# Cached attention with output projection on one core: a V block in two transfers, the last unit's turn moved ahead of the wo products, half of wo in one transfer, x in 16 rows

## The chip, the cores and the metric

The kernel runs on one core of a Trainium2 chip. The metric is the device time of one execution in microseconds (us). Other times are from one profiled execution and count from the start of its span.

The engines are called PE (matrix products; PEld is its weight load), DVE (vector), ACT (scalar), POOL and SP (which issues the DMA transfers here). The core's transfers run on 16 DMA engines.

## The reference

Eight sequences of four new tokens attend to a cache of 2048 keys and values. There are 32 query heads and 8 key/value heads of size 128; four query heads share one key/value head.

```
q = (x @ wq)                      # x [8, 4, 512], wq [512, 4096]
scores = q . k_cache * 128**-0.5  # k_cache [8, 8, 2048, 128]
p = softmax(scores)
o = p . v_cache                   # v_cache [8, 8, 2048, 128]
out = o @ wo                      # wo [4096, 512], out [8, 4, 512]
```

All arrays are bf16. K and V are 32 MiB each, wq and wo 4 MiB each, x 32 KiB: about 75.5 MB are read, and 32 KiB written.

## The kernel before, in words

The work is cut into 16 units: one sequence and four key/value heads each. A unit has 64 rows of queries (four heads, four query heads each, four tokens). K is loaded in eight transfers of 4 MiB, one for each sequence (`load_pair`, L95), that is for two units; V in blocks of 2 MiB, one for each unit (`load_v`, L100), of which the first two come as one transfer (L149). The sequence positions are spread over the partitions, so that each transfer writes 128 partitions in long runs.

For each pair of units DVE turns the K block in four pieces (`turn_keys`, L129), PE makes the scores from them (L227), DVE finds the maxima and ACT the exponentials with their sums (`softmax_top`, L245 to L263), DVE turns these (`turn_probs`, L276), and copies on ACT, POOL and DVE spread them into an array that PE can use as weights (`copy_probs`, L290). PE multiplies them with the V block in 32 products of 256 columns, in four quarters (`values`, L328). A unit's result is then divided by the sums (`divide`, L342, on ACT, for the last units on DVE), turned by a product with an identity matrix and copied into the array oT (`finish`, L352: the product at L365, for unit 15 two at L357; a copy at L366). `all_values(w, ...)` (L483) runs the four quarters of unit w, with whatever functions are handed to it after the first, second, third and fourth quarter.

When all units of one half of the heads are in oT (units that belong to the first half end with unit 13, those of the second with unit 15), `to_tokens(n)` (L373) turns that half to rows of tokens with eight products into two PSUM tiles and copies these to nat_sb with ACT and DVE; `to_wo_rows(n)` (L388) takes every eighth column of it with eight more products and copies the result to oP with ACT and DVE. `project(p, r0, n)` (L406) then multiplies rows r0 to r0+n-1 of the piece p of oP with wo: two products of 256 columns for each row, one for either half of the output. wo comes in six transfers (`pieces`, L417): two pieces of 1 MiB for the first half of the heads, and 1 MiB, 640, 256 and 128 KiB for the second half. The products go into two PSUM tiles (out_ps) that two copies (L555) take to out_sb, and one transfer stores it (L556).

The order of the instructions on each engine is that of the program text (`manual_schedule`, L71): every engine runs its own in the order in which they are written. All transfers are issued by SP, in order. SP waits before a transfer until the buffer is free, and in the trace also until a transfer further back has landed. The first wo transfer is issued at 156.03 us, when PE has read the last V block in the buffer that wo takes over; the last at 159.90 us.

The tail, from L532 on, is this: unit 12's values; unit 13's, with finish(12) inside; divide(13) on ACT; finish(13); unit 14's values, with to_tokens(0) after the first quarter and to_wo_rows(0) after the third; divide(14) on DVE; unit 15's values, with finish(14) after the second quarter; divide_all(15) on ACT; then wo products between the steps of unit 15's turn:

```
    project(0, 0, half)
    finish(NU - 1)
    project(0, half, half)
    to_tokens(1)
    project(1, 0, half)
    to_wo_rows(1)
    project(1, half, half)
    for piece in pieces[2:]:
        project(*piece)
```

x is loaded near the start (L112 to L114). With XR = 4 it lies in 8 partitions, four tokens of 1 KiB in a row, in the buffer that later takes the first V block; DVE clears this part of the buffer first, and 16 small products turn x (L141).

Of the kernel before, what the change touches and what calls it, by code (L numbers as in the profile page):

```python
# [14 lines left out]
def kernel(  # L15
# [9 lines left out]
    nc = tc.nc  # L25
# [8 lines left out]
    G = 4  # L34
    S = 128 // G
    C = Sk // S
# [5 lines left out]
    HP = 8  # L42
    WR = 8
    NP = Hq // HP
    DH = D // 2
    NU = (Hkv // G) * B
    KB, VB, PB, LAG = 2, 2, 2, 2
    NPAIR = NU // 2
    XR = 4
    scale = float(Dh) ** -0.5  # L50
    AX = mybir.AxisListType.X
    ADD = mybir.AluOpType.add
# [37 lines left out]
    vs = [v_sb[u % VB] for u in range(NU)]  # L90
# [4 lines left out]
    def load_pair(p):  # L95
        nc.sync.dma_start(
            k_sb[p % KB][:, :, :], k_cache[p].rearrange("g (s c) d -> (g s) c d", c=CP)
        )

    def load_v(u):  # L100
        v, b = units[u]
        nc.sync.dma_start(
            vs[u], v_cache[b, G * v : G * v + G].rearrange("g (s c) d -> (g s) c d", c=C)
        )

    def load_wo(p, r0, n):
        rows = wo[p * HP * 128 : (p + 1) * HP * 128, :].rearrange("(q r) j -> q r j", r=WR)
        w0 = p * WR + r0
        nc.sync.dma_start(wo_sb[:, w0 : w0 + n, :], rows[:, r0 : r0 + n, :])

    load_pair(0)
    x_all = v_sb[0][:T, :, :].rearrange("q c d -> q (c d)")[:, : XR * D]  # L112
    nc.vector.memset(x_all, 0.0)
    nc.sync.dma_start(x_all[::XR, :], x.flatten_outer_dims().rearrange("(a i) d -> a (i d)", i=XR))  # L114
    nc.sync.dma_start(wq_sb[:, :, :], wq.rearrange("(p r) n -> p r n", r=R))
# [21 lines left out]
    xtp = psum_m.tile([128, R, T], FP32, tag="m", name="xtp")  # L137
    for i in range(XR):
        row = x_all[:, i * D : (i + 1) * D].rearrange("q (p r) -> q r p", r=R)
        for r in range(R):  # L140
            nc.tensor.matmul(  # L141
                xtp[:, r, i::XR],
                lhsT=row[:, r, :],
                rhs=ident[:T, :T:XR],
                start=True,
# [153 lines left out]
    def sums(p):  # L299
        swapped = []  # L300
        for j in range(2):
            swapped.append(small.tile([128, 1], FP32, tag=f"l_swapped{j}", name="l_swapped"))
            swap_halves(nc.gpsimd, swapped[j], l_sbs[(p, j)])
        found = []
        for v in range(2):
            total = small.tile([128, 1], FP32, tag=f"l_total{v}", name="l_total")
            for i in range(4):
                rows, j = slice(i * S, (i + 1) * S), (i % 2) ^ v
                nc.gpsimd.tensor_tensor(  # L309
                    out=total[rows, :], in0=l_sbs[(p, j)][rows, :], in1=swapped[j][rows, :], op=ADD  # L310
                )
            found.append((units.index((v, p)), total))
        return found
# [8 lines left out]
    def values(u, quarter):  # L322
        if quarter == 0:
            o_pss[u] = psum_o.tile([128, 2, Dh], FP32, tag="o", name="o_ps")
        h, a0 = quarter // 2, quarter % 2 * (C // 8)
        for a in range(C // 8):
            c = quarter * C // 4 + 2 * a
            nc.tensor.matmul(  # L328
                o_pss[u][:, :, :].rearrange("n j d -> n (j d)"),
                lhsT=probs_of[u][:, h, a0 + a, :, :, :].rearrange(  # L330
                    "s j g q -> s (j g q)"
                ),
                rhs=vs[u][:, c : c + 2, :].rearrange("s c d -> s (c d)"),
                start=(c == 0),
                stop=(c == C - 2),
            )

    def divide_all(u):
        o_scs[u] = const.tile([128, 2, Dh], FP32, name="o_all")
        nc.scalar.mul(out=o_scs[u][:, :, :], in_=o_pss[u][:, :, :], mul=r_sbs[u][:, 0:1])  # L340

    def divide(u):  # L342
        o_scs[u] = small.tile([128, Dh], FP32, tag="o_sc", name="o_sc")
        for h in range(2):
            rows = slice(h * NQ, (h + 1) * NQ)
            to, of, by = o_scs[u][rows, :], o_pss[u][rows, h, :], r_sbs[u][rows, 0:1]
            if u < NU - LAG:
                nc.scalar.mul(out=to, in_=of, mul=by)  # L348
            else:
                nc.vector.tensor_scalar_mul(out=to, in0=of, scalar1=by)  # L350

    def finish(u):  # L352
        v, b = units[u]
        o_t = psum_m.tile([128, NQ], FP32, tag="m", name="o_t")
        if u == NU - 1:
            for h in range(2):
                nc.tensor.matmul(  # L357
                    o_t[:, :],
                    lhsT=o_scs[u][:, h, :],
                    rhs=ident4[:, h * NQ : (h + 1) * NQ],  # L360
                    start=(h == 0),
                    stop=(h == 1),
                )
        else:
            nc.tensor.matmul(o_t[:, :], lhsT=o_scs[u][:, :], rhs=both[:, :], start=True, stop=True)  # L365
        (nc.scalar.copy if u in (NU - 3, NU - 1) else nc.vector.tensor_copy)(  # L366
            out=oT[v][:, :, :, b, :].rearrange("d (k r) p s -> d p k r s", k=2),
            in_=o_t[:, :].rearrange("d (k p r s) -> d p k r s", k=2, p=2, s=Sq),
        )
# [3 lines left out]
    def to_tokens(n):  # L373
        half = HP // 2
        for i, copy in enumerate(two_copies):
            nat = psum_m.tile([2 * T, half, 128], BF16, tag="m", name="nat")
            for h in range(half):
                nc.tensor.transpose(  # L378
                    nat[:, h, :],
                    oT[n][:, (i ^ n) * half + h, :, :, :].rearrange("d p b s -> d (p b s)"),  # L380
                    ident[:, :],
                )
            copy(
                out=nat_sb[:, i * half * 128 : (i + 1) * half * 128],
                in_=nat[:, :, :].rearrange("t h d -> t (h d)"),
            )

    def to_wo_rows(n):  # L388
        by_row = nat_sb[:, :].rearrange("t (q r) -> t r q", r=WR)
        half = WR // 2  # L390
        for i, copy in enumerate(two_copies):
            perm = psum_m.tile([128, half, 2 * T], FP32, tag="m", name="perm")
            for r in range(half):
                nc.tensor.matmul(  # L394
                    perm[:, r, :],
                    lhsT=by_row[:, i * half + r, :],
                    rhs=ident[: 2 * T, : 2 * T],
                    start=True,
                    stop=True,
                )  # L400
            copy(
                out=oP[n][:, i * half : (i + 1) * half, :, :].rearrange("q r p t -> q r (p t)"),
                in_=perm[:, :, :],
            )

    def project(p, r0, n):  # L406
        for r in range(r0, r0 + n):
            for half in range(2):
                nc.tensor.matmul(  # L409
                    out_ps[half][half * T : (half + 1) * T, :],  # L410
                    lhsT=oP[p // 2][:, r, p % 2, :],
                    rhs=wo_sb[:, p * WR + r, half * DH : (half + 1) * DH],
                    start=(p == 0 and r == 0),
                    stop=(p == NP - 1 and r == WR - 1),
                )

    pieces = [(0, 0, 8), (1, 0, 8), (2, 0, 8), (3, 0, 5), (3, 5, 2), (3, 7, 1)]  # L417

    waiting = []

    def all_inverses():
        while waiting:
            inverses(*waiting.pop(0))
# [59 lines left out]
    def all_values(w, *between):  # L483
        for quarter in range(4):
            values(w, quarter)
            for what in between[quarter : quarter + 1]:
                if what:
                    what()

    p, w = NPAIR - 1, NU - 7  # L490
# [28 lines left out]
    all_values(w + 1)  # L519
    divide(w + 1)  # L520
    load_v(NU - 2)
    load_v(NU - 1)
    waiting += sums(p)
    all_values(NU - 5, None, lambda: finish(NU - 7))
    divide(NU - 5)
# [1 line left out]
    copy_probs(NU - 2, (nc.gpsimd.tensor_copy,))  # L527
    all_inverses()
    wo_sb = wpool.tile([128, NP * WR, D], BF16, tag="w", name="wo_sb")
    for piece in pieces:  # L530
        load_wo(*piece)
    all_values(NU - 4, lambda: finish(NU - 6), lambda: finish(NU - 5))  # L532
# [1 line left out]
    copy_probs(NU - 1, act_dve)  # L534
    all_values(NU - 3, None, lambda: finish(NU - 4))
    divide(NU - 3)
    finish(NU - 3)
    all_values(NU - 2, lambda: to_tokens(0), None, lambda: to_wo_rows(0))
    divide(NU - 2)
    all_values(NU - 1, None, lambda: finish(NU - 2))  # L540
    divide_all(NU - 1)

    out_ps = [psum_s.tile([128, DH], FP32, tag="s", name="out_ps") for _ in range(2)]
    half = WR // 2
    project(0, 0, half)
    finish(NU - 1)
    project(0, half, half)
    to_tokens(1)
    project(1, 0, half)
    to_wo_rows(1)  # L550
    project(1, half, half)
    for piece in pieces[2:]:
        project(*piece)
    for i, copy in enumerate((nc.scalar.copy, nc.vector.tensor_copy)):
        copy(out=out_sb[:, i * DH : (i + 1) * DH], in_=out_ps[i][i * T : (i + 1) * T, :])  # L555
# [31 lines left out]
```

## Time and profile before

| | us |
|---|---|
| device time, median of 3 runs | 184.58 (184.46 to 184.69) |
| device time of the profiled execution | 184.57 |
| its span | 182.70 |

| engine | busy us | share of the span |
|---|---|---|
| PE | 147.6 | 81% |
| PEld | 90.8 | 50% |
| DVE | 128.2 | 70% |
| ACT | 73.8 | 40% |
| POOL | 69.0 | 38% |

The mean granted clock of PE over the span is 0.981 of full speed. 75.73 MB are moved, at a mean of 415 GB/s.

A line of a timeline gives the start in us, the time taken in us, the engine, the line of the kernel, the operation, out<-in with the names of the tiles, the shapes, and the number of instructions merged into the line. Brackets hold the idle time of that engine just before, and what ended it. A line of the DMA issues gives out<-in, the issuing engine, the number of transfers, the KB of each and the median time from issue to landing. The page's row of slices cuts the span into 40 equal parts; a digit is the busy share in tenths, 9 is 90% or more. A busy PE is not PE at its peak, since products are pipelined: the time from one start to the next is what counts.

### The profile page before, as it was taken

How to read it: one execution, taken by the hardware profiler on the slowest of the kernel's cores; microseconds unless marked ns; L12 is line 12 of the kernel's file. 1: busy time of each engine (PE TensorE's matmuls, PEld its weight loads, DVE VectorE, ACT ScalarE, POOL GpSimd, SP SyncE). 2: the span in 40 equal slices, each digit the busy share in tenths (PEclk: the TensorE clock that was granted, in tenths of full speed). 3: DMA queues.
4: the chain of work that ended last, by engine and by line, in shares of the span. 5: the costliest groups of instructions: out<-in, count | busy, mean ns of one | idle time of the engine just before them, and what ended most of it. 6: DMA issues, size and time to landing. Idle time of an engine off the chain costs nothing.

```text
span 182.7 us, 2731 instructions
## 1 busy us (share of the span) xinstructions
PE 147.6 (81%) x1032; PEld 90.8 (50%) x1032; DVE 128.2 (70%) x170; ACT 73.8 (40%) x129; POOL 69.0 (38%) x171
## 2 busy tenths in 40 slices
PE   0019549996799799987498998978998999989993
PEld 0014114433343384563156656835853579877872
DVE  6019365879779788929799897799859659960210
ACT  2000050088060059500920892891496068682030
POOL 8900040038331237411331381572363399860000
PEclk9999996999999999999789999999999999999999
DMA  6998999999989999999989999999999999999991
GB/s 230 459 431 387 452 459 398 416 438 466 452 370 441 459 398 475 396 427 470 441 377 434 457 441 395 431 423 484 398 416 427 438 431 427 431 427 416 429 389 45
DMA packets 4524, 75.73 MB, mean 415 GB/s; under 512 B 504, under 2 KB 664, under 8 KB 928
## 3 DMA queue, kind: packets, MB, share of 16 engines
q1 hardware_dynamic: 4512, 75.57, 96.9%
q8 instruction: 8, 0.13, 0.3%
q14 instruction: 4, 0.03, 0.0%
HBM read 75.53 MB, written 0.03 MB: 414 GB/s over the span
## 4 chain that ended last, share of the span: by engine, by line
DMA 42%; DVE 30%; PE 14%; issue 6%; ACT 4%; POOL 1%; SPq 1%; ACTq 0%; DVEq 0%
DMA k_sb<-in_k_cache_dram 27%; DVE kt L129 21%; DMA k_sb<-in_v_cache_dram 16%; PE o_ps L328 8%; DVE top L245 5%; ACT s_sb L263 3%; PE s_ps L227 2%; PE out_ps L409 2%; DVE p_t L276 2%; DVE swapped L237 1%; ACT probs L290 1%; DVE less L251 1%; PE perm L394 1%; POOL probs L290 1%; PE nat L378 1%
## 5 line engine op out<-in xcount | busy, mean ns | idle before, releaser
L129 DVE STREAM_TRANSPOSE kt<-k_sb 128x2048 f32<-128x2048 f32 x32 | 71.5, 2278 | 16.3 <-DMA k_sb<-in_k_cache_dram 13.9
L328 PEld LDWEIGHTS <-probs 128*128 128x128 bf16 x448 | 42.4, 99 | 15.2 <-issue 8.2
L227 PE MATMUL s_ps<-kt,q_bd 128*64 128x512 bf16 x256 | 36.9, 403 | 15.1 <-DVE kt L129 8.9
L263 ACT ACTIVATE s_sb<-s_ps,less 128x1024 bf16<-128x1024 f32 x16 | 22.4, 1401 | 58.5 <-DVE less L251 26.6
L290 POOL COPY probs<-p_t 32x512 bf16<-32x512 bf16 x48 | 29.1, 606 | 34.0 <-PE o_ps L328 31.9
L157 PE MATMUL unread<-ident 128*128 128x512 f32 (+1 forms) x86 | 40.0, 610 | 0.0
L290 ACT COPY probs<-p_t 32x512 bf16<-32x512 bf16 x52 | 32.0, 616 | 1.3 <-DVE p_t L276 0.3
L227 PEld LDWEIGHTS <-q_bd 128*64 128x64 bf16 x256 | 15.7, 112 | 32.9 <-issue 18.9
L157 PEld LDWEIGHTS unread<-ident 128*128 128x128 f32 x86 | 16.2, 198 | 18.6 <-issue 18.5
L328 PE MATMUL o_ps<-v_both,probs 128*128 128x256 bf16 x192 | 23.0, 273 | 0.9 <-DMA v_both<-in_v_cache_dram 0.8
L245 DVE TENSOR_REDUCE top<-s_ps 128x1 f32<-128x1024 f32 x16 | 19.4, 1212 | 4.7 <-PE s_ps L227 4.7
L328 PE MATMUL o_ps<-v_more,probs 128*128 128x256 bf16 x160 | 19.8, 277 | 0.0
L237 POOL COPY l_swapped<-l_sb 64x1 f32<-64x1 f32 x32 | 6.5, 204 | 32.2 <-ACT s_sb L263 31.3
L276 DVE STREAM_TRANSPOSE p_t<-s_sb 128x512 f32<-128x512 f32 x16 | 11.3, 708 | 6.0 <-ACT s_sb L263 6.0
L348 ACT ACTIVATE o_sc<-o_ps,r_sb 64x128 f32<-64x128 f32 x28 | 10.1, 360 | 10.9 <-PE o_t L365 7.7
L309 POOL TENSOR_TENSOR l_total<-l_sb,l_swapped 32x1 f32<-32x1 f32 x64 | 11.8, 184 | 4.0
L328 PE MATMUL o_ps<-k_sb,probs 128*128 128x256 bf16 x96 | 11.6, 272 | 0.2 <-DMA k_sb<-in_v_cache_dram 0.2
L141 PE MATMUL xtp<-ident,v_both 32*128 32x8 bf16 x16 | 0.7, 174 | 13.1 <-DMA v_both<-in_x_dram 13.1
L181 ACT ACTIVATE q_nat<-psq 128x512 bf16<-128x512 f32 x2 | 1.2, 598 | 22.1 <-PE psq L170 22.1
L290 POOL COPY last_probs<-p_t 32x512 bf16<-32x512 bf16 x12 | 8.1, 673 | 0.6
L196 POOL COPY q_bd<-q_t 32x512 bf16<-32x512 bf16 x3 | 1.9, 646 | 16.7 <-DVE q_t L190 16.6
L290 DVE COPY probs<-p_t 32x512 bf16<-32x512 bf16 x12 | 7.9, 661 | 0.3
(47 smaller groups left out, 83.9 us busy)
## 6 DMA issues: line engine op xcount, KB each, us to landing
k_sb<-in_k_cache_dram SPq DMA_DIRECT2D x8, 4096.0 KB, 19.9
v_more<-in_v_cache_dram SPq DMA_DIRECT2D x6, 2048.0 KB, 25.0
v_both<-in_v_cache_dram SPq DMA_DIRECT2D x4, 2048.0 KB, 22.6
k_sb<-in_v_cache_dram SPq DMA_DIRECT2D x4, 2048.0 KB, 24.8
wq_sb<-in_wq_dram SPq DMA_DIRECT2D x1, 4096.0 KB, 19.9
v_both<-in_v_cache_dram SPq DMA_DIRECT2D x1, 4096.0 KB, 29.6
wo_sb<-in_wo_dram SPq DMA_DIRECT2D x3, 1024.0 KB, 19.1
wo_sb<-in_wo_dram SPq DMA_DIRECT2D x1, 640.0 KB, 21.1
```

The source lines that it names most:

```text
L129: nc.vector.transpose(kts[(p, t)][:, :, :, :, :, :].rearrange("k c w j s e -> k (c w j s e)").bitcast(FP32), k_sb[p % KB][:, t * CT : (t + ...
L157: nc.tensor.matmul(unread[:, :, :], lhsT=ident4[:, :], rhs=ident4[:, :].unsqueeze(1).broadcast_to([128, width, 128]), start=True, stop=True,)
L227: nc.tensor.matmul(s_pss[(p, j)][h * NQ : (h + 1) * NQ, t // 2, :, :], lhsT=q_bd[:, j, k, e, p, :, :].rearrange("k g q -> k (g q)"), rhs=k ...
L237: engine.tensor_copy(out=out[h * NQ : (h + 1) * NQ, :], in_=in_[(1 - h) * NQ : (2 - h) * NQ, :])
L245: nc.vector.reduce_max(out=top[:, :], in_=s_pss[u][:, :, :, :].rearrange("q i c s -> q (i c s)"), axis=AX,)
L263: nc.scalar.activation(out=s_sbs[u][:, :, :, :].rearrange("q a w j -> q a j w"), in_=s_pss[u][:, :, :, :].rearrange("q i c s -> q c s i"), ...
L276: nc.vector.transpose(p_ts[u][:, :, :, :, :].rearrange("s x g q j -> s (x g q j)").bitcast(FP32), s_sbs[u][:, :, :, :].rearrange("q a s j ...
L290: by[x * G + col](out=probs_of[u][rows, x, :, :, col, :], in_=p_ts[(b, j)][quad * S : (quad + 1) * S, :, col % 2, :, :].rearrange("s x q j ...
L309: nc.gpsimd.tensor_tensor(out=total[rows, :], in0=l_sbs[(p, j)][rows, :], in1=swapped[j][rows, :], op=ADD)
L328: nc.tensor.matmul(o_pss[u][:, :, :].rearrange("n j d -> n (j d)"), lhsT=probs_of[u][:, h, a0 + a, :, :, :].rearrange("s j g q -> s (j g q)"),
L348: nc.scalar.mul(out=to, in_=of, mul=by)
L409: nc.tensor.matmul(out_ps[half][half * T : (half + 1) * T, :], lhsT=oP[p // 2][:, r, p % 2, :], rhs=wo_sb[:, p * WR + r, half * DH : (half ...
```

## The change

Four things change.

- x is laid in 16 partitions with two tokens in each (XR = 2), and so in rows of 2 KiB; the cleared part of the buffer and the number of products that turn it follow from XR.
- Unit 15's V block is loaded in two transfers, the first and the second half of the runs of each partition. The other blocks are loaded as before.
- The two wo pieces of the first half of the heads are loaded in one transfer of 2 MiB; the runs of 8 KiB are the same. The other four pieces stay.
- In the tail, finish(13) moves into unit 14's values, after the second quarter; to_tokens(0) moves from after the first quarter to after the third, and to_wo_rows(0) from after the third quarter to behind divide(14). After unit 15's values the turn of unit 15 (finish, to_tokens) comes at once. Four of the sixteen rows of the first half's wo products (eight products) stay between to_tokens(1) and to_wo_rows(1), all others come after to_wo_rows(1).

```diff
-    XR = 4
+    XR = 2
...
-    def load_v(u):
+    def load_v(u, c0=0, n=C):
         v, b = units[u]
-        nc.sync.dma_start(
-            vs[u], v_cache[b, G * v : G * v + G].rearrange("g (s c) d -> (g s) c d", c=C)
-        )
+        blocks = v_cache[b, G * v : G * v + G].rearrange("g (s c) d -> (g s) c d", c=C)
+        nc.sync.dma_start(vs[u][:, c0 : c0 + n, :], blocks[:, c0 : c0 + n, :])
...
+    def load_first_half_of_wo():
+        p = NP // 2
+        nc.sync.dma_start(
+            wo_sb[:, : p * WR, :].rearrange("q (p r) j -> q p (r j)", p=p),
+            wo[: p * HP * 128, :].rearrange("(p q r) j -> q p (r j)", p=p, r=WR),
+        )
...
-    pieces = [(0, 0, 8), (1, 0, 8), (2, 0, 8), (3, 0, 5), (3, 5, 2), (3, 7, 1)]
+    pieces = [(2, 0, 8), (3, 0, 5), (3, 5, 2), (3, 7, 1)]
...
     load_v(NU - 2)
-    load_v(NU - 1)
+    for c0 in (0, C // 2):
+        load_v(NU - 1, c0, C // 2)
...
     wo_sb = wpool.tile([128, NP * WR, D], BF16, tag="w", name="wo_sb")
+    load_first_half_of_wo()
     for piece in pieces:
         load_wo(*piece)
...
     divide(NU - 3)
-    finish(NU - 3)
-    all_values(NU - 2, lambda: to_tokens(0), None, lambda: to_wo_rows(0))
+    all_values(NU - 2, None, lambda: finish(NU - 3), lambda: to_tokens(0))
     divide(NU - 2)
+    to_wo_rows(0)
     all_values(NU - 1, None, lambda: finish(NU - 2))
     divide_all(NU - 1)
 
     out_ps = [psum_s.tile([128, DH], FP32, tag="s", name="out_ps") for _ in range(2)]
-    half = WR // 2
-    project(0, 0, half)
     finish(NU - 1)
-    project(0, half, half)
     to_tokens(1)
-    project(1, 0, half)
+    project(0, 0, WR // 2)
     to_wo_rows(1)
-    project(1, half, half)
-    for piece in pieces[2:]:
+    project(0, WR // 2, WR // 2)
+    project(1, 0, WR)
+    for piece in pieces:
         project(*piece)
```

## The prediction, made before the changed kernel ran

> **What bounds the kernel now.** I read the page first: engine shares, the slices, the DMA queues.
>
> ```profile
> DMA  6998999999989999999989999999999999999991
> ...
> q1 hardware_dynamic: 4512, 75.57, 96.9%
> q8 instruction: 8, 0.13, 0.3%
> ```
>
> The DMA row is full in 38 of 40 slices, and the loads' queue takes 96.9% of sixteen engines' span. So the time can change in two ways only: the bytes take longer or shorter, or something happens behind the last landing. I therefore went to the end, first with the DMA issues and their times to landing in narrow windows (line, size in KB, us from issue to landing).
>
> ```profile
> k_sb<-in_v_cache_dram SPq DMA_DIRECT2D x1, 2048.0 KB, 24.7
> ```
>
> ```profile
> wo_sb<-in_wo_dram SPq DMA_DIRECT2D x1, 128.0 KB, 19.6
> ```
>
> The first is unit 14's V block, issued at 140.00: it lands at 164.7. Unit 15's, issued at 144.83, takes 24.8: 169.6. The second is the last wo piece, issued at 159.90: it lands at 179.5. The same view gives the wo pieces before it: 174.5 for (1,0,8), 177.0 for (2,0,8), 178.5 for (3,0,5), 179.1 for (3,5,2). Then the timeline of the tail (start, us, engine, line; in brackets the idle time before).
>
> ```profile
> 160.02 1.91 PE L328 MATMUL o_ps<-k_sb,probs 128*128 128x256 bf16 x16 [0.19 <-DMA k_sb<-in_v_cache_dram]
> ...
> 164.72 0.43 PE L365 MATMUL o_t<-both,o_sc 128*128 128x64 f32 x2 [0.88 <-ACT o_sc L348]
> ...
> 164.99 1.04 PE L328 MATMUL o_ps<-k_sb,last_probs 128*128 128x256 bf16 x8
> ...
> 169.88 1.91 PE L328 MATMUL o_ps<-k_sb,probs 128*128 128x256 bf16 x16
> ...
> 173.63 0.61 PE L409 MATMUL out_ps<-wo_sb,oP 128*32 128x256 bf16 x8
> 173.74 0.48 ACT L340 ACTIVATE o_all<-o_ps,r_sb 128x256 f32<-128x256 f32 x1 [4.52 <-PE o_ps L328]
> ...
> 174.27 0.66 PE L357 MATMUL o_t<-ident,o_all 128*128 128x64 f32 x4
> ...
> 174.96 0.21 ACT L366 CAST oT<-o_t 128x64 bf16<-128x64 f32 x1 [0.75 <-PE o_t L357]
> ...
> 175.40 0.63 PE L378 MATMUL nat<-ident,oT 128*64 128x128 bf16 x8
> ...
> 175.90 0.58 ACT L383 COPY nat_sb<-nat 64x512 bf16<-64x512 bf16 x1 [0.73 <-PE nat L378]
> ...
> 176.63 0.66 PE L394 MATMUL perm<-ident,nat_sb 64*128 64x64 bf16 x8
> ...
> 177.22 2.56 PE L409 MATMUL out_ps<-wo_sb,oP 128*32 128x256 bf16 x40
> ...
> 179.50 0.09 PEld L409 LDWEIGHTS <-oP 128*32 128x32 bf16 x1 [0.17 <-issue]
> 179.80 0.36 ACT L555 CAST out_sb<-out_ps 32x256 bf16<-32x256 f32 x1 [2.35 <-PE out_ps L409]
> ```
>
> The reader is to see that two limits meet here. The last pair of wo products starts at 179.50, when the last piece lands. But PE was almost as late: from 164.99 on it hardly pauses, and the last 40 products (20 pairs, since each row r has one for either half of the output, and the two run side by side) start at 177.22 and follow each other at 0.109 us a pair, as the trace's single records show. Unhindered, the twentieth would start at 177.23 + 19 x 0.109 = 179.30. So **PE's slack against the last landing is 0.2 us**: whatever PE does later than 0.2 us is paid in full, whatever it does earlier is worth nothing beyond the landing.
>
> **The change, part by part.** All is reckoned against the profiled execution, span 182.70 and 184.57 us in all; the median of the runs is 184.58, so a difference carries over directly.
>
> *Order in the tail.* Prices first. A value product takes 0.109 us ((1.91 - 0.27) / 15 from the row of 16). A finish between values costs 0.17 (171.62 to 171.79). to_tokens(0) costs 0.66 (164.99 + 8 x 0.109 = 165.87; the next value row is at 166.53), to_wo_rows(0) 0.72 (166.53 + 16 x 0.109 = 168.27 to 168.99).
> 1. finish(13) leaves the head of unit 14. PE now goes from unit 13 straight to unit 14's V block. That lands at 164.73; unit 13's landed at 159.88 and its first product started at 160.02, so unit 14 starts at about 164.87 instead of 164.99: 0.12 earlier. (Bounds: nothing gained, or 0.2.)
> 2. finish(13) comes back inside unit 14: +0.17. to_tokens(0) and to_wo_rows(0) move but stay in front of unit 15. Their casts and copies on ACT and DVE have 0.8 us of values or more beside them. The DVE copy of to_wo_rows(0) now queues behind divide(14), 0.71 us; the next reader of that buffer is finish(15), four microseconds on.
> 3. So the last value product starts at 173.43 - 0.12 + 0.17 = 173.48, 0.05 later.
> 4. Unit 15 "at once". divide_all 0.48, finish(15), the cast of oT: this chain waited for nothing before either. The eight wo products at 173.63 lay under o_all and ended before it. So the cast ends at 175.18 + 0.05 = 175.23 and to_tokens(1) starts at about 175.28. Before, it started at 175.40, held up by the wo products put before it. Gain 0.12.
> 5. The nat copies and to_wo_rows(1) follow as before, still with eight wo products under the copies: perm at 176.51, its next product at 177.11.
> 6. Behind to_wo_rows(1) there now stand 4 + 8 + 8 + 5 + 2 + 1 = 28 pairs, not 20: of the wo products that filled PE's waits for ACT, eight pairs have lost their cover, and PE stands idle in those waits instead. The last pair starts at 177.11 + 27 x 0.109 = 180.06.
> Against 179.50 that is **+0.56 us**. The output casts, the store and the end follow unchanged (179.80 to 182.70 before).
>
> *Unit 15's V block in two transfers.* In the trace's packet records a packet of 16 KiB takes 0.611 us and one of 8 KiB 0.309, so eight of the former become sixteen of the latter on each engine: +0.056 us, and 0.009 for one more semaphore write. The first half would land some 2.4 us before the second; but PE reaches unit 15 at 169.88 with no pause before it, so it is not waiting for the block now. The second half's wait is new on PE, ahead of unit 15's third quarter, with everything after it queued behind; it lands at about 169.7 to 169.8, PE gets there at about 171.8. Worth nothing; the 0.06 falls on the wo landings, which are no longer last. If they were, it would cost 0.06.
>
> *First half of wo in one transfer.* Same 8 KiB runs, one semaphore write and one issue (0.4 us of SP) fewer. It lands where its second piece did, 174.5, and is first read at about 175.85. SP's last wo issue waited until 159.90 for unit 13's V block, eight transfers back; one transfer more and one fewer leave that distance at eight. Nothing.
>
> *x in 16 rows.* The memset on DVE halves (0.91 us) and 16 small matmuls become 8 (0.66 us in all); both lie in the first 14 us, before DVE and PE have anything but the first K load to wait for. What can matter is the engines' load. Before, the records show eight packets of 4 KiB, 0.159 each, on eight engines; the other eight had none. A packet of 2 KiB takes 0.084. The nearest row for the spread is the output store, 32 rows with 16 semaphore writes: so all sixteen engines get one, 0.093 with its semaphore write. An engine that had x is 0.075 earlier for the rest of the run, one that hadn't 0.093 later. Unit 14's block is complete when its latest engine is; followed back through the semaphore writes, the latest two are engines without an x packet. I take **+0.09** on the landing from which step 1 starts, bounds -0.08 and +0.09.
> The Trainium skill, "DMA: Bandwidth & Descriptors", section "Why a DMA increments its semaphore by 16 and not by 1", has a rule for this: the number of engines is the largest up to 16 that divides the slowest dimension of both sides. By it 8 rows go to 8 engines, as the trace has it, and 16 rows to 16, which gives the same +0.09; were it still 8 engines with two packets each, it would be +0.01.
>
> **Sum:** 184.57 + 0.56 + 0.09 = **185.2 us**. With the bounds of steps 1 and 4 (0.1 to 0.15 either way) and x's: 184.9 to 185.4.
>
> **The rivals.**
> - *The landing stays the bound.* If PE gets through the tail half a microsecond faster than I reckon, the last piece sets the end as now, later by 0.06 and 0.09: 184.7. For it: the slack is small, and one wait that I misread in steps 1 to 5 would do. Against: the 28 pairs are counted, and their 0.109 is read from twenty of their kind. 0.19.
> - *Faster, by the instruction fetches.* The queue of kind "instruction" carries eight 16 KiB fetches. In the records a fetch throws the engine that carries it back by 1.42 us for good: seven hit before the last wo piece, and the sixteen engines' semaphore writes of one transfer, 0.46 us apart at first, end 1.76 apart. The latest engines are hit ones. PE has 16 instructions fewer ahead, so fetches fall elsewhere; if, in the stretch to 164.7, they cease to hit engines that are late already, landings come up to 1.3 us earlier and PE with them: 185.2 - 1.3 = 183.9. It decides from 0.7 us on. Against: eight engines are late, and all must be spared. 0.06.
> The Trainium skill, "Runtime: NRT & Kernel Launch", section "Instruction fetch mechanics", calls the cost of crossing such a block mostly hidden; by that, this rival would be worth nothing. For PE the trace agrees, for the DMA engines it doesn't (1.42 us).
> - *PE's clock drops*, since fillers went: the pairs would take twice 0.109, +3 us, 188. The granted clock is 1.00 in every window from 156 on, over an idle 0.88 us at 163.84; the new pauses are about 0.6. 0.02.
> - *The change does not do what it says:* the eight pairs are still under the waits. The code has them behind to_wo_rows(1); no chance of its own.
>
> **How the numbers follow.** Forecast 0.73, landing 0.19, fetches 0.06, clock 0.02. The range 184.6 to 185.5 holds the forecast's own and the landing rival, some 0.87. A measurement tells 0.2% from no change, 0.37 us: faster below 184.21, slower above 184.95. The forecast's own range lies a little across that line (0.04 of it). So faster 0.06, same 0.23, slower 0.71.
>
> **What would show it.** Right: unit 14's first value at about 164.95; nat at 175.35; a run of 56 wo products starting near 177.2 without a pause, ending near 180.4; the last pair at about 180.15, with the last piece landed at 179.65. Wrong: a pause before the last pair (then the landing is still the bound), a first value of unit 14 well before 164.8 (then step 1), or a granted clock below 1.00 in the last 10 us.

## The result, and the profile after

The changed kernel takes 185.07 us, the median of five executions (185.00 to 185.31), against 184.57 before (8 executions, 184.45 to 184.69). The ratio is 1.0026, 95% interval 1.0015 to 1.0037: slower by 0.28 to 0.68 us. The profiled execution has 185.31 us, the longest of the five, and a span of 183.5. Of the 65 executions on record of kernels with x in 16 rows 25 took 187 to 196 us, three of the changed kernel's eight among them, and none of the 131 of kernels with x in 8 rows did: why is not known, and they are left out of the times given here.

The page of the changed kernel, the rows that were shown of before:

```profile
DMA  6999999999999899989999999999999999999980
...
q1 hardware_dynamic: 4656, 75.57, 96.5%
q8 instruction: 8, 0.13, 0.3%
```

The queue is as full as it was, but the last of the 40 slices now reads 0: the loads end further ahead of the end of the span. The landings, in the same narrow windows (KB, us from issue to landing): unit 14's V block, issued at 140.47, then wo's first half, issued at 156.51, and wo's last piece, issued at 160.24.

```profile
k_sb<-in_v_cache_dram SPq DMA_DIRECT2D x1, 2048.0 KB, 24.6
```

```profile
wo_sb<-in_wo_dram SPq DMA_DIRECT2D x1, 2048.0 KB, 18.4
```

```profile
wo_sb<-in_wo_dram SPq DMA_DIRECT2D x1, 128.0 KB, 19.6
```

That is 165.1, 174.9 and 179.8 (165.05, 174.89 and 179.88 without the rounding of the rows). The timeline of the changed kernel's tail:

```profile
165.18 1.91 PE L334 MATMUL o_ps<-k_sb,last_probs 128*128 128x256 bf16 x16 [1.00 <-DMA k_sb<-in_v_cache_dram]
...
166.92 0.33 PE L371 MATMUL o_t<-both,o_sc 128*128 128x64 f32 x2
...
170.22 1.92 PE L334 MATMUL o_ps<-k_sb,probs 128*128 128x256 bf16 x16
...
174.10 0.47 ACT L346 ACTIVATE o_all<-o_ps,r_sb 128x256 f32<-128x256 f32 x1 [3.65 <-PE o_ps L334]
...
174.62 0.66 PE L363 MATMUL o_t<-ident,o_all 128*128 128x64 f32 x4 [0.56 <-ACT o_all L346]
...
175.58 0.63 PE L384 MATMUL nat<-ident,oT 128*64 128x128 bf16 x8 [0.30 <-ACT oT L372]
...
176.15 0.61 PE L415 MATMUL out_ps<-wo_sb,oP 128*32 128x256 bf16 x8
...
176.82 0.65 PE L400 MATMUL perm<-ident,nat_sb 64*128 64x64 bf16 x8
...
177.40 3.23 PE L415 MATMUL out_ps<-wo_sb,oP 128*32 128x256 bf16 x56
...
180.67 0.36 ACT L561 CAST out_sb<-out_ps 32x256 bf16<-32x256 f32 x1 [3.03 <-PE out_ps L415]
```

Two things carry the result. PE now idles 0.56 and 0.30 us for ACT in unit 15's turn, where wo products lay before. And 56 products instead of 40 follow to_wo_rows(1), without a pause: 3.23 us, the last pair at 180.36, half a microsecond after the last piece has landed (before, it started at 179.50, when the last piece landed). The bound has gone from the landing to PE.

### The profile page after: what moved, and what is told of

It reads as the page before. It is cut to its first block, busy times and chain, and to the rows that moved or that the text cites. A ratio compares the mean times of both kernels' runs of the same rounds, so it can differ in the third digit from the quotient of the medians.

```text
span 183.5 us, 2717 instructions
## 1 busy us (share of the span) xinstructions
PE 146.6 (80%) x1024; PEld 90.8 (49%) x1024; DVE 127.8 (70%) x170; ACT 73.8 (40%) x129; POOL 69.0 (38%) x171
## 4 chain that ended last, share of the span: by engine, by line
DMA 53%; DVE 27%; PE 10%; ACT 3%; issue 3%; POOL 1%; SPq 1%; ACTq 0%; DVEq 0%
DMA k_sb<-in_k_cache_dram 40%; DVE kt L135 19%; DMA k_sb<-in_v_cache_dram 13%; PE o_ps L334 5%; DVE top L251 4%; ACT s_sb L269 3%; PE out_ps L415 2%; DVE p_t L282 2%; PE s_ps L233 1%; DVE swapped L243 1%; DVE less L257 1%; PE perm L400 1%; POOL probs L296 1%; PE nat L384 1%; PE o_t L363 0%
## 5 line engine op out<-in xcount | busy, mean ns | idle before, releaser
L233 PE MATMUL s_ps<-kt,q_bd 128*64 128x512 bf16 x256 | 35.2, 388 | 16.4 <-DVE kt L135 9.2
L163 PE MATMUL unread<-ident 128*128 128x512 f32 (+1 forms) x86 | 40.9, 623 | 0.0
```

Of the source, the lines that this page charges most:

```text
L163: nc.tensor.matmul(unread[:, :, :], lhsT=ident4[:, :], rhs=ident4[:, :].unsqueeze(1).broadcast_to([128, width, 128]), start=True, stop=True,)
L233: nc.tensor.matmul(s_pss[(p, j)][h * NQ : (h + 1) * NQ, t // 2, :, :], lhsT=q_bd[:, j, k, e, p, :, :].rearrange("k g q -> k (g q)"), rhs=k ...
```

## The experiments

Theory: the end is set by the later of two times, the last wo landing and the end of PE's tail, which moves by 0.109 us for each pair behind to_wo_rows(1). Rival: the later landings make the difference, and PE only follows. The first four runs take the change apart.

**e1: only the order of the tail.**

```diff
-    finish(NU - 3)
-    all_values(NU - 2, lambda: to_tokens(0), None, lambda: to_wo_rows(0))
+    all_values(NU - 2, None, lambda: finish(NU - 3), lambda: to_tokens(0))
     divide(NU - 2)
+    to_wo_rows(0)
...
-    project(0, 0, half)
     finish(NU - 1)
-    project(0, half, half)
     to_tokens(1)
-    project(1, 0, half)
+    project(0, 0, WR // 2)
     to_wo_rows(1)
-    project(1, half, half)
+    project(0, WR // 2, WR // 2)
+    project(1, 0, WR)
```

> The kernel before with only the new order of the tail: x in 8 rows, V block 15 in one transfer, wo in six. Theory (PE's late products set the end): 28 pairs behind to_wo_rows(1) instead of 20, and nothing later on the DMA side: +0.56 us, 185.1. Rival (the later landings set the end, PE only follows them): nothing landed later, so 184.6, and the last pair still starts when the last wo piece lands.

Measured: ratio 1.0030 (1.0018 to 1.0042); six of eight executions at 185.02 to 185.26, which is 0.47 to 0.71 above before's 184.55. The theory's 0.56 is there with all loads as they were. Two executions, the profiled one among them, took 186.63 and 186.76: see PE's clock, in the last section.

**e2: everything but the order of the tail** (the whole diff without e1's).

> The changed kernel with the old order of the tail: x in 16 rows, V block 15 in two transfers, first half of wo in one. Theory: the last landing is the bound again and comes later by 0.09 (x) and 0.06 (V in 8 KiB packets): +0.15 us, 184.7. Rival (landings): the whole difference is here, +0.5 us, 185.1.

Measured: 185.08 to 185.29, ratio 1.0039 (1.0026 to 1.0051). The theory's 184.7 failed: the time is the one that the rival gave, although e1 shows the order alone to cost as much. Together the two would make some 1.2 us, and the changed kernel has 0.5; so something in the loads costs in the old order only. e4 and e8 name it.

**e3: only x in 16 rows.**

```diff
-    XR = 4
+    XR = 2
```

> The kernel before with only x in 16 rows of 2 KiB. Theory: +0.09 us on the last landing, which is the bound: 184.65, the sixteen engines finishing x within 0.5 us of each other. Rival (x's earlier issue, 1.41 instead of 1.94 us, disturbs the first K packets): the first K block lands some 0.3 us later, as in the changed kernel's profile (13.24 against 12.89 us for its first reader), and the time is +0.4 us, 185.0.

Measured: 184.61 to 184.78, ratio 1.0007 (0.9997 to 1.0018). That agrees with 0.09 and excludes the rival's 0.4, but it does not exclude zero. In the packet records of the one profiled execution the last semaphore write of the wo loads is at 179.30 us, in before's at 179.11; the landings are at 179.59 and 179.46.

**e4: the changed kernel, with the wo products put back between the steps of unit 15's turn.**

```diff
+    project(0, 0, WR // 2)
     finish(NU - 1)
+    project(0, WR // 2, WR // 2)
     to_tokens(1)
-    project(0, 0, WR // 2)
+    project(1, 0, WR // 2)
     to_wo_rows(1)
-    project(0, WR // 2, WR // 2)
-    project(1, 0, WR)
+    project(1, WR // 2, WR // 2)
```

> The changed kernel with the wo products of the first half put back between the steps of unit 15's turn (20 pairs behind to_wo_rows(1)); the moves of finish(13), to_tokens(0) and to_wo_rows(0) and all loads stay changed. Theory: the last landing is the bound again, 0.15 us later than before: 184.7 to 184.8. Rival (landings set the changed kernel's end): no gain against the changed kernel, 185.1 to 185.3.

Measured: 185.05 to 185.38, ratio 1.0042 (1.0030 to 1.0054): the theory's 184.7 to 184.8 failed. The timeline of e4 says why:

```profile
174.77 0.61 PE L415 MATMUL out_ps<-wo_sb,oP 128*32 128x256 bf16 x8 [0.78 <-DMA wo_sb<-in_wo_dram]
...
175.31 0.66 PE L363 MATMUL o_t<-ident,o_all 128*128 128x64 f32 x4
```

The first eight wo products wait 0.78 us for wo, because its first half now lands as one, and unit 15's finish is queued behind them on PE. If that is what the merge does, it delays the old order and not the new one, in which nothing reads wo so early; e8 and e10 test this. So e2 and e4 carried a wait of their own and can't tell the theories apart. The next four runs keep wo in six transfers, or merge it alone.

**e5, e6, e7: e1 with 20, 24 and 32 pairs behind to_wo_rows(1)** (e1 has 28). The lines of e5, e6 and e7 that stand for e1's:

```
# e5
    project(0, 0, WR // 2)
    finish(NU - 1)
    project(0, WR // 2, WR // 2)
    to_tokens(1)
    project(1, 0, WR // 2)
    to_wo_rows(1)
    project(1, WR // 2, WR // 2)
# e6
    project(0, 0, WR // 2)
    finish(NU - 1)
    to_tokens(1)
    project(0, WR // 2, WR // 2)
    to_wo_rows(1)
    project(1, 0, WR)
# e7
    finish(NU - 1)
    to_tokens(1)
    to_wo_rows(1)
    project(0, 0, WR)
    project(1, 0, WR)
```

> The kernel before with finish(13), to_tokens(0) and to_wo_rows(0) moved as in the change, but the wo products left between the steps of unit 15's turn: 20 pairs behind to_wo_rows(1); all loads as before. Theory (pairs behind to_wo_rows(1) times 0.109 us): PE could start the last pair at 177.28 + 19 x 0.109 = 179.35, before the last landing at 179.50, so no difference, 184.6. Rival (the moves of unit 13's and 14's steps cost the time): 185.1 as with the whole new order.

> As the last, but only four pairs lie under divide_all(15) and four between to_tokens(1) and to_wo_rows(1): 24 pairs behind it. Theory: last pair at 177.11 + 23 x 0.109 = 179.62, +0.12 us: 184.7. Rival (only whether the turn comes at once matters, not the number of products behind it): it lies with the 28 pairs, 185.1, or with the 20, 184.55.

> As the last, but no wo product before to_wo_rows(1): 32 pairs behind it. Theory: last pair at 177.11 + 31 x 0.109 = 180.49, +0.99 us: 185.55. Rival (only the turn's place matters): 185.1, as with 28.

| pairs behind to_wo_rows(1) | forecast us over before | measured (medians over 184.52; e1: its six lowest over 184.55) | ratio, interval |
|---|---|---|---|
| 20 (e5) | 0 | -0.01 | 0.9997 (0.9989 to 1.0006) |
| 24 (e6) | 0.12 | 0.07 | 1.0003 (0.9994 to 1.0012) |
| 28 (e1) | 0.56 | 0.58 | 1.0030 (1.0018 to 1.0042) |
| 32 (e7) | 0.99 | 0.96 | 1.0053 (1.0039 to 1.0067) |

A flat part while the landing is the bound, then a slope of 0.89 / 8 = 0.11 us a pair from 24 to 32. Neither rival of these runs is left: the place of unit 15's turn is not what counts, and the moves of unit 13's and 14's steps cost nothing (e5). The row of wo products in e5, e6 and e7, one kernel each:

```profile
177.25 2.50 PE L409 MATMUL out_ps<-wo_sb,oP 128*32 128x256 bf16 x40
```

```profile
177.00 2.80 PE L409 MATMUL out_ps<-wo_sb,oP 128*32 128x256 bf16 x48
```

```profile
177.29 3.67 PE L409 MATMUL out_ps<-wo_sb,oP 128*32 128x256 bf16 x64
```

Forty products in a row without a wait would take 0.27 + 19 x 0.109 = 2.34 us, so e5's 2.50 contain a wait for the last landing; sixty-four would take 0.27 + 31 x 0.109 = 3.65, so e7's contain none.

**e8: only wo's first half in one transfer**, in the old order.

```diff
-    pieces = [(0, 0, 8), (1, 0, 8), (2, 0, 8), (3, 0, 5), (3, 5, 2), (3, 7, 1)]
+    pieces = [(2, 0, 8), (3, 0, 5), (3, 5, 2), (3, 7, 1)]
...
+    load_first_half_of_wo()
     for piece in pieces:
         load_wo(*piece)
...
-    for piece in pieces[2:]:
+    for piece in pieces:
         project(*piece)
```

> The kernel before with only the first half of wo in one transfer. Theory: the half lands as a whole at 174.5 where its first piece landed at 172.1; the wo products at 173.63 now wait for it until 174.65, and finish(15) with all behind it stands queued behind them on PE: the twentieth pair moves from an unhindered 179.30 to about 180.3, +0.8 us, 185.35. Rival (the merge costs nothing, as the prediction had it for the new order): 184.55.

Measured: 185.14 to 185.39, ratio 1.0041 (1.0029 to 1.0054), 0.76 us. The wait in its timeline:

```profile
174.53 0.61 PE L416 MATMUL out_ps<-wo_sb,oP 128*32 128x256 bf16 x8 [0.75 <-DMA wo_sb<-in_wo_dram]
...
178.03 2.36 PE L416 MATMUL out_ps<-wo_sb,oP 128*32 128x256 bf16 x40
```

The first wo products start 0.9 us later than before's 173.63, and the forty products 0.8 later than 177.22, now without a wait for their own landing (2.36 us, where 2.34 were worked out above).

**e9 to e12: do the parts add up?** The changed kernel again; the changed kernel with wo in six transfers; that with 20 pairs (e4's diff); the kernel before with only unit 15's V block in two transfers. The edit of e10, against the changed kernel, and that of e12, against the kernel before (with load_v as in the change):

```diff
-    pieces = [(2, 0, 8), (3, 0, 5), (3, 5, 2), (3, 7, 1)]
+    pieces = [(0, 0, 8), (1, 0, 8), (2, 0, 8), (3, 0, 5), (3, 5, 2), (3, 7, 1)]
...
-    load_first_half_of_wo()
...
-    for piece in pieces:
+    for piece in pieces[2:]:
         project(*piece)
```

```diff
-    load_v(NU - 1)
+    for c0 in (0, C // 2):
+        load_v(NU - 1, c0, C // 2)
```

> The changed kernel once more, beside the next three. Theory: order +0.56 us and, since PE's tail hangs on the landing of unit 14's V block, x in 16 rows +0.09: 185.2. Rival (x adds nothing here): as with the new order alone, 185.1. In the profile, unit 14's first value product starts as much later than 164.99 - 0.12 as its block lands later than 164.73.

> The changed kernel with the first half of wo in two transfers as before. Theory: in the new order nothing reads wo before 175.8, so the merge is worth nothing and costs nothing there: within 0.05 us of the changed kernel. Rival (the merge saves issue or transfer time): 0.1 us or more slower than the changed kernel.

> As the last, with the wo products put back between the steps of unit 15's turn: 20 pairs behind to_wo_rows(1). x in 16 rows, the split V block and the moves of unit 13's and 14's steps stay. Theory: the last landing is the bound again, 0.09 (x) and 0.06 (V) later than before: 184.7, half a microsecond less than the changed kernel. Rival (the loads cost the time): 185.1.

> The kernel before with only unit 15's V block in two transfers. Theory: sixteen 8 KiB packets for eight of 16 KiB on each engine and one more semaphore write, all on the last landing: +0.06 us, 184.6; unit 15's first value still follows unit 14's last without a pause. Rival (the half that lands earlier lets unit 15 start earlier): its first value well before 169.8 and a time below 184.4.

Measured: e9 has five executions at 184.98 to 185.21, and 186.83 (profiled) and 186.92; e10 five at 185.13 to 185.24, and 186.84 and 186.89. Their intervals, 1.0022 to 1.0068 and 1.0061 to 1.0133, take in the latter and longer ones, so I compare the five lowest of each, which is a weaker comparison. By their medians, 185.11 and 185.16, the merge is worth 0.05 us in the new order, no more than the five of one kernel differ. Over its before (184.53) the changed kernel has 0.58 us, as e1 has over its own: x's 0.09 doesn't show behind PE's tail. e11, with all of x and V but 20 pairs: 184.65 to 184.99, median 0.27 over before (interval of the ratio 1.0003 to 1.0059, which takes in a longer execution too). That is nearer to the 0.15 expected than to the 0.58, but the highest of its six just reaches the lowest of e9's five. e12: ratio 1.0009 (1.0000 to 1.0017), 0.14 us against 0.06 expected. Its unit 15 starts no earlier:

```profile
169.08 1.05 PE L327 MATMUL o_ps<-k_sb,last_probs 128*128 128x256 bf16 x8
169.96 1.91 PE L327 MATMUL o_ps<-k_sb,probs 128*128 128x256 bf16 x16
```

Unit 15's first product follows unit 14's eighth after 169.96 - 169.08 = 0.88 us, the eight products' own time. No kernel tried is faster than the one before; e5 equals it.

## Why the prediction was right

- **What bounds the kernel:** right. Both limits met within 0.2 us, and e5 and e6 show the flat part that this makes.
- **Steps 1 and 2, unit 14's start:** predicted 164.96 with x's share, measured 165.18 in the profiled execution, 0.14 after a landing at 165.05 instead of 164.82. In e1, with x as before, it was 164.90, where 164.87 was reckoned. The rule (the landing plus 0.14) held. The landing varies by more than I allowed: unit 14's first product lies between 164.77 and 165.18 over eight profiled executions in which finish(13) is moved (the changed kernel, e1, e4 to e7, e9, e10), and 165.08 is reached with x in 8 rows too (e7).
- **Steps 3 to 5:** right to some 0.02 us. From unit 14's first value to the last value 8.61 us were reckoned and 8.61 measured; to to_tokens(1) 10.41 and 10.40; to the products behind to_wo_rows(1) 12.24 and 12.22.
- **Step 6, the 28 pairs:** right, and the heart of it (e1, e5 to e7).
- **V block in two transfers:** worth nothing, as reckoned. Where the landing is the bound (e12) the time is 0.14 us longer (0.00 to 0.31), which takes in the 0.06 reckoned.
- **wo in one transfer:** nothing, and right for this order: it landed at 174.9 and was first read at 176.15, and e10 shows no difference beyond the spread. That the same edit costs 0.76 us in the old order I had not seen when I set up e2 and e4.
- **x in 16 rows:** the packets came as forecast, sixteen of 2 KiB (0.084 us each) near 12 us in the changed kernel's packet records, where before has eight of 4 KiB. The 0.09 us is not shown: e3 agrees with it but doesn't exclude zero, and e9's five lowest and e1's six lowest are alike. The forecast of 0.65 us is 0.15 above the 0.50 measured, and this term can be part of it; but e9, the same kernel, has 0.58, and single executions start and land too unevenly to settle 0.09 us.
- **The rivals:** that the landing stays the bound is excluded by e1, and the fetches didn't help: unit 14's block and the last piece landed later than before, not earlier. "PE's clock drops", to which I gave 2 in 100, was priced too low in chance: it happens in some executions, as the last section shows, and adds some 1.6 us, not 3. The reason that I gave against it, the full clock over an idle 0.88 us, did not carry over. That none of the five executions behind the 185.07 had it is luck: two of the seven of e9, the same kernel, had it.

## What to carry to other kernels

Where a transfer's landing and an engine's backlog end together, a reorder is priced by what stands behind the last dependency, not by how early the dependency is met: count the instructions behind it and multiply by their spacing. Independent products lie best in the waits of the dependent chain, as they did here before the change. Here each pair behind cost 0.11 us, once the landing no longer covered it. And a merged transfer moves the landing of its first part: ask who reads that part first, and what is queued behind the reader on its engine. In e8 that was worth 0.76 us.

## What the runs showed of the hardware that I had not expected

PE's clock can halve although PE made no pause longer than 0.57 us in the 3.4 us before. In the profiled execution of e1 (186.63 us) the granted clock is 0.50 from 177.0 to 180.4, just over the wo products. Two windows of e1 (us; busy time of PE, PEld, DVE, ACT and POOL with the number of instructions; granted clock; DMA share; GB/s), and under them the same products:

```profile
173.55:176.97 3.42, 2.50 (x30) 1.77 (x28) 0.42 (x1) 1.26 (x3) 0.00 (x0) 1.00 0.99 414
176.97:180.38 3.41, 3.41 (x36) 2.50 (x36) 0.42 (x1) 0.37 (x1) 0.00 (x0) 0.50 0.43 162
```

```profile
177.15 4.79 PE L409 MATMUL out_ps<-wo_sb,oP 128*32 128x256 bf16 x56
```

That is 4.79 us instead of the changed kernel's 3.23 for the same 56 products: a pair takes 0.213 us while the clock is halved, by the trace's single records, and 0.109 otherwise. The same stretch before the drop, in the kernel before:

```profile
173.55:176.97 3.42, 3.34 (x44) 2.30 (x43) 0.42 (x1) 1.27 (x3) 0.00 (x0) 1.00 0.98 412
```

With the wo products in the waits PE is busy 3.34 of 3.42 us, without them 2.50. The kernels with 28 pairs have six executions near 186.6 to 186.9, with a mean granted clock of 0.942 to 0.952 over the span, among some 27; no execution of before, e5 or e6 is above 185, and e7's five, with 32 pairs, lie at 185.40 to 185.65. The Trainium skill, "TensorE: Matmul & The Clock Gate", Part 1, has the clock halved after an idle window of about 3.4 us. The length of the half-clock stretch agrees (3.41 us), but the window ahead of it was 73% busy (2.50 of 3.42).

That share alone does not decide. In each kept trace the changes of the clock lie whole multiples of 3.413 us apart. On that grid, over the fourteen kept traces, PE was busy for at most 42% of the window in 30 of the 32 windows behind which a full clock halved, and for at least 44% in all 602 behind which it stayed full. The other two are these drops, e1's at 73% and e9's at 74%. The changed kernel's profiled execution has 2.56 of 3.42 us busy (75%) from 172.95 to 176.37 and e7 has 2.49 of 3.41 (73%) from 174.50 to 177.91, both on the grid, and no drop. What sets these two windows apart stays open.
